# Sparse attention and two feed-forward layers on one core: later additions for pairs 12 to 15, a load on another queue, and an earlier end of odd pairs' first sums

## The chip, the cores and the metric

The program runs on one core of a Trainium2 chip. The metric is the time of one execution on the device, in microseconds (us), as the median of several runs. The trace of the kernel before is one profiled execution. Its engines are PE (TensorE; PEld is its weight load), DVE (VectorE), ACT (ScalarE), POOL (GpSimd) and SP, which computes nothing here and only issues DMAs. Every engine works through its own instructions in order, so an instruction that waits holds up all that stand behind it on that engine, the DMAs that the engine issues among them.

## The reference

Four batches of 576 tokens with 8 heads of 64 go through an attention in which only scores within `tau` of the row's maximum count. Its output is the input of a gated layer (d_ff 1536), and that one's output of a second layer (d_ff 1024) with a softmax-weighted activation and a layer norm. All of it is float32.

```python
def _attn_ref(q, k, v, tau):
    scores = (1.0 / np.sqrt(q.shape[-1])) * np.matmul(q, k.transpose(0, 1, 3, 2))
    thresh = np.max(scores, axis=-1, keepdims=True) - tau
    scores = np.where(scores >= thresh, scores, -1000000000.0)
    attn = np.exp(scores - np.max(scores, axis=-1, keepdims=True))
    attn = attn / (np.sum(attn, axis=-1, keepdims=True) + 1e-09)
    return np.matmul(attn, v)

def _moe_ref(x, w_a, w_b, w_out):          # x: attention output, 2304 x 512
    return ((x @ w_a) * (x @ w_b)) @ w_out

def _moe2_ref(x, w_in, w_out, g_ln):
    h = x @ w_in
    e = np.exp(h - np.max(h, axis=-1, keepdims=True))
    solu = h * (e / (np.sum(e, axis=-1, keepdims=True) + 1e-09))
    ln = (solu - mean(solu)) / np.sqrt(var(solu) + 1e-06) * g_ln
    return ln @ w_out
```

## The kernel before

**Attention** treats two heads at a time: 16 pairs, four of each batch, each in 9 slices of scores. The loop over `m` (78 steps) handles two slices a step, in an order written out by hand in `PROG`. In a step PE makes the scores (L684); DVE scales them and takes their maxima (`ns`, L689); ACT takes the exponential (`pe`, L701); POOL turns the maximum into a threshold (`th`, L706, 128 numbers); DVE masks by it (L715). Thresholds of the two slices stand early in a step's POOL work. PE transposes what the step before masked (L735), ACT copies it out of PSUM (`pt`, L728), and PE multiplies it with V (L787). There are no scores after step 71; steps 72 to 77 finish the last pairs.

The product with V of a pair comes in two sums, 1 and 2, which use one PSUM buffer `po` in turn. The table `PV` says in which step, counted from the pair's first, which part of which sum is multiplied: one entry for even pairs, one for odd ones. At the end of the step in which a sum is complete, ACT copies it to `xp` (L795), ahead of that step's copies `pt`. `xp` has two buffers, so pair j+2 takes the one of pair j.

**The result x** goes to DRAM (`xd`, one tensor for each batch) in two halves: SP writes the first half of a pair (L797) in the step after its second sum, and POOL later adds the second half (L798, a DMA with `accum_op=add`), behind the bulk work of its step. The addition waits until SP's write has landed. In the kernel before it is issued two steps after the pair's second sum is complete: for pairs 12, 13, 14 and 15 at the ends of steps 63, 68, 72 and 77.

**Blocks of x.** The layer after the attention takes x in three blocks of 768 columns. Block 0 (batches 0 and 1) is loaded in step 46, block 1 (batches 1 and 2) from step 65 on, both on SP: `load_z` (the reciprocal sums, L454) and `load_x` (L470, and for each new batch 512 runs of two numbers into `vs`, L473). From step 69 on, one instruction of block 1's normalization is put on DVE in each step, ahead of the step's masks; the first needs `vs`. Block 2 (the rest of batch 2 and all of batch 3, pairs 8 to 15) is loaded by SP behind the loop, with `load_x(2)`. The next instructions that SP issues then belong to the layer: stores of operands (`opd<-xt`, L554) and loads of raw weights (`wraw`, L200, two buffers). Block 2 is multiplied by its reciprocal sums much later (POOL, L492, 327.70 us).

**The gated layer** (`moe1`) runs 36 rounds of seven products each (L611) over three PSUM buffers that ACT and DVE empty. The order is planned in the program's own build by the times of a small model of the engines; `product` is called by the attention's step 72 for the first three.

Of the kernel before, what the change touches and what calls it, by code (L numbers as in the profile page):

```python
# [14 lines left out]
ALU = mybir.AluOpType  # L15
# [6 lines left out]
def kernel(  # L22
# [11 lines left out]
    nc = tc.nc  # L34
# [3 lines left out]
    S = SM + D  # L38
# [33 lines left out]
    xd = [dram.tile([P, KC, S + 2], F32, name=f"xd{b}") for b in range(B)]  # L72
# [23 lines left out]
    vs = {}  # L96
# [339 lines left out]
    def cuts(p, c0, c1):  # L436
        o, got = 0, []
        for b, s0, s1 in SEG[p]:
            a, z = max(o, c0), min(o + s1 - s0, c1)
            if a < z:  # L440
                got.append((b, s0 + a - o, a - c0, z - a))
            o += s1 - s0
        return got
# [13 lines left out]
    def alloc_x(p):  # L457
        if p == 2:
            xr = pools["w4"].tile([P, 7 * 2 * QK * P], F32, tag="w", name="x2")
            xr = xr[:, 0:KC * 2 * H].rearrange("p (k c) -> p k c", k=KC)  # L460
        else:
            xr = raw_p.tile([P, KC, 2 * H], F32, name="xr0")
        xs[p] = xr

    def load_x(p):
        if p not in xs:
            alloc_x(p)
        xr = xs[p]
        for b, s0, c, m in cuts(p, 0, 2 * H):
            nc.sync.dma_start(out=xr[:, :, c:c + m], in_=xd[b][:, :, s0:s0 + m])  # L470
            if b not in vs:
                vs[b] = const.tile([P, KC, 2], F32, name=f"vs{b}")
                nc.sync.dma_start(out=vs[b], in_=xd[b][:, :, S:S + 2])  # L473
                vnew.append(b)

    def norm_ops(p, whole=True):
# [153 lines left out]
    def attention():  # L630
        es, es_r = ExitStack(), ExitStack()
        slots, late, bulk, adds = [], [], [], []
# [21 lines left out]
        def alloc_qk(i):  # L654
            q = pq.tile([P, 2, S], F32, name="q")
            k = pq.tile([P, 2, HS + D], F32, name="k")
            ld[i] = (q, k)
# [114 lines left out]
        def pv(i, r, ka, kz):  # L772
            n = R1 if r == 1 else R2 + 2
            if ka == 0:
                st[i, "o", r] = ps_a.tile([P, 2, 512], F32, name="po", bufs=1)
            po = st[i, "o", r][:, :, 0:n]
            vr = ld[i, "v"]

            def mm(kc, h, g):
                rows = slice(g * D, (g + 1) * D)  # L780
                if kc < NQ:
                    lhsT, rhs = vr[rows, h * NQ + kc], dt[h, r][rows, kc, 0:n]
                elif g == h:
                    lhsT, rhs = vr[rows, 2 * NQ], dt["t", r][rows, 0:n]
                else:
                    return
                nc.tensor.matmul(po[h * D:(h + 1) * D, g], lhsT=lhsT, rhs=rhs, start=(kc == 0), stop=(kc == NQ - (g != h)), skip_group_check=True)  # L787

            def store():
                b, hp = divmod(i, NPAIR)  # L790
                if r == 1:
                    st[i, "x"] = px.tile([P, 2, S + 2], F32, name="xp")
                xp = st[i, "x"]
                c0 = 0 if r == 1 else R1
                nc.scalar.activation(out=xp[:, :, c0:c0 + n], in_=po, func=AF.Copy)  # L795
                if r == 2:
                    dma_q.append(lambda: nc.sync.dma_start(out=xd[b][:, hp, :], in_=xp[:, 0]))  # L797
                    adds.append((m + 2, lambda: nc.gpsimd.dma_start(out=xd[b][:, hp, :], in_=xp[:, 1], accum_op=ALU.add)))  # L798

            if kz == NQ + 1:  # L800
                pv_q.append(store)
            return [lambda kc=kc, h=h, g=g: mm(kc, h, g) for kc in range(ka, kz) for g in range(2) for h in range(2)]
# [14 lines left out]

            pv_q.append(store)

        PV = ({4: (1, 0, 3), 5: (1, 3, 5), 6: (2, 0, 2), 7: (2, 2, 5)}, {4: (1, 0, 2), 5: (1, 2, 4), 6: (1, 4, 5), 7: (2, 0, 3), 8: (2, 3, 5)})  # L820
        alloc_qk(0)
        q0, k0 = ld[0]
        def first_k(eng, h, g):
# [21 lines left out]
        tot = NP * NS  # L845
# [26 lines left out]
        for m in range(tot // 2 + 6):  # L872
            if m == 46:
                load_z(0)
                load_x(0)
                ops = {"n": [[x] for x in norm_ops(0)], "s": sum_ops(0, 0, True), "z": [[("S", 0, lambda: load_z(1))]], "x": [[("S", 0, lambda: load_x(1))]]}
                ops["h"], ops["l"] = zip(*(operand_ops(0, j, 0, True) for j in range(NX)))
                ops["o"] = [[("S", 0, lambda j=j: store_op(0, j, 0))] for j in range(NX)]
                slots = [[x for w in st.split() for x in ops[w[0]][int(w[1])]] for st in STEPS]
                late = norm_ops(1)  # L880
# [8 lines left out]
            lo_old, lo_q = lo_q, []  # L889
            pvs = [(j,) + PV[j % 2][m - j * NS // 2] for j in range(max(0, 2 * m // NS - 2), min(NP, 2 * m // NS + 1)) if m - j * NS // 2 in PV[j % 2]]  # L890
            mms = [f for p in pvs for f in pv(*p)]
# [111 lines left out]
        for fn in dma_q + [fn for _, fn in adds] + later:  # L1003
            fn()
        later.clear()
        load_x(2)
        es.close()

    yt = {}
# [456 lines left out]
    with tc.manual_schedule():  # L1466
        mhalf = const.tile([P, 1], F32, name="mhalf")
        nc.gpsimd.memset(mhalf, -0.5)
        attention()
        pools["ps"] = es_t.enter_context(tc.tile_pool(name="ps_t", bufs=4, space=PSUM))  # L1470
        pools["wo"] = ctx.enter_context(tc.tile_pool(name="wo", bufs=2 * F1))
        moe1()
        moe2()
# [56 lines left out]
```

## Time and profile before

| What | Value |
|---|---|
| Median of 3 runs | 912.55 us (912.37 to 912.76) |
| The profiled execution | 912.18 us, of which its span is 910.4 us |
| Busy in the span: PE, DVE | 880.8 us (97%), 692.0 us (76%) |
| Busy in the span: ACT, POOL | 542.4 us (60%), 175.0 us (19%) |
| Mean granted clock of TensorE | 0.994 |

The profiled execution lies 1.8 us over its span. A clock of 1.00 in a row is 2.4 GHz, 0.50 is 1.2 GHz. Attention takes the first 280 us or so of the span, the gated layer runs to about 700 us and the second layer to the end. Busy shares count an instruction from its start to its end, so PE at 97% is not PE at its peak.

### The profile page before, as it was taken

The page shows a single profiled execution, that of the slowest core. Times are in us where ns is not written, and L with a number is a line of the kernel's source. Part 1 is how long each engine was busy: PE and PEld are TensorE (multiplying, and loading weights), DVE is VectorE, ACT ScalarE, POOL GpSimd, SP SyncE. Part 2 cuts the span into 40 slices and gives each one's busy share as a digit, 9 for nine tenths or more (in the row PEclk, how much of TensorE's full clock was granted, in tenths as well). Part 3 has the DMA queues.
Part 4 walks back from the last instruction along what each step waited for, and adds up shares of the span by engine and source line. Part 5 has one row for each costly group of instructions (what it writes and reads, how often), then busy time and mean ns, then how long its engine had stood idle before and what let it go on. Part 6 is the DMA issues. An engine that isn't in the chain of part 4 may idle for free.

```text
span 910.4 us, 17279 instructions
## 1 busy us (share of the span) xinstructions
PE 880.8 (97%) x6354; PEld 742.6 (82%) x6354; DVE 692.0 (76%) x1508; ACT 542.4 (60%) x1041; POOL 175.0 (19%) x309
## 2 busy tenths in 40 slices
PE   7999999999979799999999999999999999999998
PEld 4566666656647799999999999999999778888886
DVE  6989898899966778886576755876644898888873
ACT  5899988879955464554454444544444566555543
POOL 1243542125312010001111121112114000000000
PEclk9999999999989999999999999999999999999999
DMA  6455454766754669569965998579869111110001
GB/s 176 139 150 170 109 164 130 200 184 200 220 152 142 232 211 362 168 235 367 313 159 116 251 346 274 113 176 308 250 143 197 38 35 59 47 47 24 24 23 47
DMA packets 71027, 152.50 MB, mean 168 GB/s; under 512 B 8736, under 2 KB 39072, under 8 KB 70944
## 3 DMA queue, kind: packets, MB, share of 16 engines
q1 hardware_dynamic: 57472, 131.83, 42.7%
q0 software_dynamic: 12672, 18.90, 13.8%
q8 instruction: 50, 0.82, 0.4%
q10 hardware_dynamic: 800, 0.68, 0.3%
q14 instruction: 33, 0.27, 0.1%
HBM read 98.06 MB, written 53.32 MB: 166 GB/s over the span
## 4 chain that ended last, share of the span: by engine, by line
PE 80%; DVE 7%; DMA 4%; ACT 4%; issue 2%; SPq 1%; POOL 0%; ACTq 0%; POOLq 0%; DVEq 0%
PE acc L611 26%; PE py L1130 16%; PE po L1424 10%; PE ph L1303 9%; PE po L787 6%; PE ps L684 5%; PE tp L735 5%; DVE pe L715 2%; DVE ns L689 2%; DMA xd<-xp 2%; PE pl L1401 2%; DMA xt<-opd 1%; ACT pe L701 1%; DMA wraw<-in_w_dram 1%; PE ps L769 1%
## 5 line engine op out<-in xcount | busy, mean ns | idle before, releaser
L611 PE MATMUL acc<-xt,w 128*128 128x384 f32 x1446 | 272.5, 338 | 5.6 <-ACT c L1218 2.7
L611 PEld LDWEIGHTS acc<-xt,w 128*128 128x128 f32 x1446 | 255.7, 189 | 7.2 <-DVE xt L237 3.6
L1108 POOL DMA_DIRECT2D yd<-y x68 | 58.8, 889 | 306.8 <-ACT y L1104 306.8
L701 ACT ACTIVATE pe<-ns,nm 128x576 f32<-128x576 f32 x128 | 94.3, 781 | 38.2 <-DVE ns L689 38.1
L715 DVE SCALAR_TENSOR_TENSOR pe<-ns,th,pe 128x576 f32<-128x576 f32 x128 | 100.4, 814 | 12.6 <-POOL th L706 6.4
L689 DVE TENSOR_SCALAR_CACHE_REDUCE ns<-ps 128x576 f32<-128x576 f32 x144 | 103.2, 751 | 7.4 <-PE ps L684 6.6
L1424 PE MATMUL po<-w,lt 128*128 128x512 f32 x432 | 103.5, 395 | 0.0
L684 PE MATMUL ps<-k,q 64*64 64x288 f32 x1152 | 93.6, 431 | 5.1 <-DMA k<-in_qkv_dram 3.3
L1424 PEld LDWEIGHTS po<-w,lt 128*128 128x128 f32 x432 | 79.9, 188 | 16.7
L1104 ACT ACTIVATE y<-py 128x384 f32<-128x384 f32 x92 | 45.0, 490 | 77.4 <-PE py L1130 74.4
L1130 PE MATMUL py<-ga,wo 128*128 128x384 f32 x432 | 84.0, 335 | 0.0
L1130 PE MATMUL py<-gb,wo 128*128 128x384 f32 x432 | 84.0, 335 | 0.0
L728 ACT ACTIVATE pt<-tp 128x512 f32<-128x512 f32 (+1 forms) x160 | 78.7, 556 | 2.1 <-PE tp L735 1.9
L787 PE MATMUL po<-pt,vr 64*64 64x322 f32 (+1 forms) x1024 | 77.2, 407 | 2.1 <-ACT xp L795 1.6
L1130 PEld LDWEIGHTS py<-ga,wo 128*128 128x128 f32 x432 | 75.7, 188 | 0.0
L1130 PEld LDWEIGHTS py<-gb,wo 128*128 128x128 f32 x432 | 75.7, 188 | 0.0
L1303 PE MATMUL ph<-w,ys 128*128 128x512 f32 x297 | 74.5, 394 | 0.7 <-ACT h L1307 0.7
L706 POOL TENSOR_SCALAR th<-nm,toff 128x1 f32<-128x1 f32 x144 | 49.4, 353 | 127.7 <-DVE ns L689 123.5
L735 PE MATMUL tp<-ident,pe 128*128 128x128 f32 x512 | 70.8, 280 | 0.0
L735 PEld LDWEIGHTS tp<-ident,pe 128*128 128x128 f32 x512 | 58.7, 144 | 11.0 <-issue 5.5
L684 PEld LDWEIGHTS ps<-k,q 64*64 64x64 f32 x1152 | 36.3, 136 | 37.5 <-issue 8.4
L1303 PEld LDWEIGHTS ph<-w,ys 128*128 128x128 f32 x297 | 55.7, 188 | 13.6 <-ACT h L1307 1.1
(156 smaller groups left out, 1215.4 us busy)
## 6 DMA issues: line engine op xcount, KB each, us to landing
xt<-opd SPq DMA_DIRECT2D x42, 768.0 KB
wraw<-in_w_dram SPq DMA_DIRECT2D x36, 512.0 KB
opd<-xt SPq DMA_DIRECT2D x21, 768.0 KB
yd<-y POOLq DMA_DIRECT2D x68, 192.0 KB, 5.5
q<-in_qkv_dram SPq DMA_DIRECT2D x15, 576.0 KB
k<-in_qkv_dram SPq DMA_DIRECT2D x30, 176.0 KB
xd<-xp SPq DMA_DIRECT2D x16, 289.0 KB
xd<-xp POOLq DMA_DIRECT2D x16, 289.0 KB, 5.4
```

Of the source, the lines that this page charges most:

```text
L611: nc.tensor.matmul(ps, lhsT=w[:, WOP[j], wi, c * P:(c + 1) * P], rhs=x[:, c, xi, :], start=(k == 0 and j < 3), stop=(k == 3 * QK - 1 and j ...
L684: nc.tensor.matmul(ps[t * D:(t + 1) * D, g, 0:HS], lhsT=q[r, u, c], rhs=k[r, u, o:o + HS], start=True, stop=True, skip_group_check=True)
L689: nc.vector.tensor_scalar(out=ns, in0=st[i, s][:, :, 0:HS], scalar1=-SCALE, scalar2=None, op0=ALU.mult, op1=ALU.min, accum_out=nm)
L701: nc.scalar.activation(out=pe.rearrange("p (g s) -> p g s", g=2), in_=ns, func=AF.Exp, bias=nm, scale=-1.0)
L715: last_mask[0] = nc.vector.scalar_tensor_tensor(out=pv, in0=ns, scalar=th, in1=pv, op0=ALU.is_le, op1=ALU.mult, accum_out=z[:, s:s + 1])
L728: evac_q.append(lambda: nc.scalar.activation(out=out, in_=in_, func=AF.Copy))
L735: nc.tensor.transpose(tp[:, kc, :], pe[:, o:o + P], ident)
L787: nc.tensor.matmul(po[h * D:(h + 1) * D, g], lhsT=lhsT, rhs=rhs, start=(kc == 0), stop=(kc == NQ - (g != h)), skip_group_check=True)
L1108: nc.gpsimd.dma_start(out=to[:, g["oc"], :], in_=y, accum_op=ALU.add)
L1130: nc.tensor.matmul(g["py"], lhsT=wos[g["q"] * F1 + r][:, wi, oc * P:(oc + 1) * P], rhs=g["g"][r][:, gi, :], start=(r == c == 0), stop=last ...
L1303: nc.tensor.matmul(ps, lhsT=v[:, a, c * P:(c + 1) * P], rhs=w[:, b], start=(k == 0 and j < 3), stop=(k == 3 * QK - 1 and j in (2, 4, 6)), ...
L1424: nc.tensor.matmul(po, lhsT=lt[:, a, j, :], rhs=w2(j, b), start=(k == 0), stop=(k == 3 * NJ - 1))
```

## The change

Four edits. The addition of a pair's second half of x is issued four steps after its second sum, instead of two, from step 60 on (pairs 12 and 13: ends of steps 65 and 70), and behind the loop for those complete in step 70 or later (pairs 14 and 15). `load_x(2)` is issued by GpSimd, behind these two additions. In the odd pairs the part of the first sum that was multiplied in the seventh step (the last 2 matmuls, 4 instructions) moves to the sixth, so that its copy to `xp` moves too.

```diff
-    def load_x(p):
+    def load_x(p, eng=nc.sync):
...
-            nc.sync.dma_start(out=xr[:, :, c:c + m], in_=xd[b][:, :, s0:s0 + m])
+            eng.dma_start(out=xr[:, :, c:c + m], in_=xd[b][:, :, s0:s0 + m])
...
-                nc.sync.dma_start(out=vs[b], in_=xd[b][:, :, S:S + 2])
+                eng.dma_start(out=vs[b], in_=xd[b][:, :, S:S + 2])
...
-                    adds.append((m + 2, lambda: nc.gpsimd.dma_start(out=xd[b][:, hp, :], in_=xp[:, 1], accum_op=ALU.add)))
+                    adds.append((m + (2 if m < 60 else 4) if m < 70 else tot, lambda: nc.gpsimd.dma_start(out=xd[b][:, hp, :], in_=xp[:, 1], accum_op=ALU.add)))
...
-        PV = (..., {4: (1, 0, 2), 5: (1, 2, 4), 6: (1, 4, 5), 7: (2, 0, 3), 8: (2, 3, 5)})
+        PV = (..., {4: (1, 0, 2), 5: (1, 2, 5), 7: (2, 0, 3), 8: (2, 3, 5)})
...
-        load_x(2)
+        load_x(2, nc.gpsimd)
```

## Rows read from the trace of the kernel before

**Rows 1.** Page, part 4: shares of the chain that ended last, by engine.

```profile
PE 80%; DVE 7%; DMA 4%; ACT 4%; issue 2%; SPq 1%; POOL 0%; ACTq 0%; POOLq 0%; DVEq 0%
```

**Rows 2.** Chain of waits, 170 to 345 us: start, us, what.

```profile
249.90 8.16 DMA xd<-xp
...
290.36 7.92 DMA wraw<-in_w_dram
...
300.59 5.98 PE acc L611 x24
...
317.34 4.16 PE acc L611 x24
```

**Rows 3.** Timeline, POOL: start, us, instruction, [idle before <- what ended it].

```profile
234.37 0.89 POOL L798 DMA_DIRECT2D xd<-xp  x1
...
240.58 1.00 POOL L237 TENSOR_TENSOR xt<-xr,xt 128x384 fp32r<-128x384 f32 x1 [1.44 <-DVE pe L715]
...
258.60 0.89 POOL L798 DMA_DIRECT2D xd<-xp  x1 [9.87 <-DMA xd<-xp]
```

**Rows 4.** Timeline, DVE, 225 to 310 us, the same columns.

```profile
235.61 0.82 DVE L715 SCALAR_TENSOR_TENSOR pe<-ns,th,pe 128x576 f32<-128x576 f32 x1 [0.44 <-POOL th L706]
...
255.57 0.23 DVE L480 TENSOR_SCALAR vs<-vs,neg 128x8 f32<-128x8 f32 x1 [3.92 <-DMA vs<-xd]
...
259.85 0.82 DVE L715 SCALAR_TENSOR_TENSOR pe<-ns,th,pe 128x576 f32<-128x576 f32 x1 [3.00 <-POOL th L706]
...
283.52 0.69 DVE L223 SCALAR_TENSOR_TENSOR st_a<-wraw,st_a 128x512 uint32<-128x512 uint32 x1
```

**Rows 5.** Timeline, SP's DMA queue: start, us spent issuing, what is issued.

```profile
243.00 2.77 SPq L473 DMA_DIRECT2D vs<-xd  x1
...
249.90 0.39 SPq L797 DMA_DIRECT2D xd<-xp  x1
...
281.95 6.41 SPq L470 DMA_DIRECT2D x<-xd  x2
...
290.36 0.83 SPq L200 DMA_DIRECT2D wraw<-in_w_dram  x2
```

**Rows 6.** Windows: length, busy us (count) PE PEld DVE ACT POOL, clock, DMA share, GB/s.

```profile
254.00:256.00 2.00, 2.00 (x28) 0.90 (x20) 0.43 (x2) 0.02 (x1) 0.00 (x0) 1.00 0.99 388
...
260.00:262.00 2.00, 0.00 (x0) 0.00 (x0) 2.00 (x5) 0.00 (x0) 0.04 (x1) 0.50 1.03 145
...
300.00:304.00 4.00, 3.41 (x11) 3.41 (x12) 2.55 (x7) 2.42 (x5) 0.00 (x0) 0.57 0.02 8
```

**Rows 7.** Tile xd: time from issue to landing of the DMAs on POOL's queue.

```profile
DMA to landing us min/median/max: 4.1/5.4/8.1
```

**Rows 8.** Timeline, ACT, 225 to 310 us.

```profile
249.74 0.59 ACT L795 ACTIVATE xp<-po 128x512 f32<-128x512 f32 x1
...
298.36 0.66 ACT L216 ACTIVATE st_a<-wraw 128x512 f32<-128x512 f32 x1 [3.44 <-DMA wraw<-in_w_dram]
```

**Rows 9.** Timeline, PE, 225 to 310 us.

```profile
274.76 0.65 PE L787 MATMUL po<-ptt,vr 64*64 64x256 f32 x4
...
276.11 2.40 PE L787 MATMUL po<-pt,vr 64*64 64x322 f32 x32 [0.70 <-ACT xp L795]
...
300.59 6.14 PE L611 MATMUL acc<-xt,w 128*128 128x384 f32 x25 [2.71 <-ACT c L1218]
```

**Rows 10.** Waits of PE's weight loads, 20 to 250 us: us, times, longest.

```profile
PEld po L787 <- ACT xp L795: 4.8, 9, 1.1
```

**Rows 11.** Timelines, PEld and ACT, in step 37, where pair 7 ends its first sum.

```profile
136.85 0.86 PEld L735 LDWEIGHTS tp<-ident,pe 128*128 128x128 f32 x8 [0.38 <-ACT pt L728]
...
138.97 1.29 PEld L787 LDWEIGHTS po<-pt,vr 64*64 64x64 f32 x24 [0.40 <-ACT xp L795]
...
136.98 1.46 ACT L701 ACTIVATE pe<-ns,nm 128x576 f32<-128x576 f32 x2 [0.21 <-DVE ns L689]
```

**Rows 12.** Timeline, DVE, in step 28, where pair 5 ends its first sum.

```profile
106.54 0.82 DVE L715 SCALAR_TENSOR_TENSOR pe<-ns,th,pe 128x576 f32<-128x576 f32 x1 [0.98 <-ACT pe L701]
```

More of the change, by code (lines that the diff above doesn't have):

```diff
@@ L818, in finish @@
             pv_q.append(store)
-        PV = ({4: (1, 0, 3), 5: (1, 3, 5), 6: (2, 0, 2), 7: (2, 2, 5)}, {4: (1, 0, 2), 5: (1, 2, 4), 6: (1, 4, 5), 7: (2, 0, 3), 8: (2, 3, 5)})
+        PV = ({4: (1, 0, 3), 5: (1, 3, 5), 6: (2, 0, 2), 7: (2, 2, 5)}, {4: (1, 0, 2), 5: (1, 2, 5), 7: (2, 0, 3), 8: (2, 3, 5)})
         alloc_qk(0)
```

## The prediction, made before the changed kernel was run

> **What bounds the kernel now.** First the page's chain: by engine, 80% of it is PE, and only DVE, DMA and ACT have a few per cent each [rows 1]. So time can come only from places where PE stops. The chain in order of time says where: around the end of the attention it runs through a write of x, 8.16 us, and a load of raw weights, 7.92 us [rows 2]. Then the waits there, engine by engine.
>
> First stop, step 68 to 69: POOL stood 9.87 us in front of pair 13's addition, until SP's write of that pair had landed [rows 3]. That write was issued at 249.90, because SP had been held in its queue by block 1's loads (the issue of `vs` alone took 2.77 us), and landed 8.16 us later [rows 2, 5]. Behind the addition stood step 69's thresholds, and DVE waited 3.00 us for them. But this is the second wait of that step: just before, DVE had waited 3.92 us for `vs`, until 255.57 [rows 4]. Taking the addition away gives back 3.00 us, not 9.87.
>
> Second stop, 298 to 300 us: SP's `load_x(2)` took from 281.95 to 288.36, since its second part waits for pair 15's addition, and the weights behind it were issued at 290.36 only [rows 5]. ACT waited 3.44 us for them, and PE, for a copy behind that on ACT, 2.71 us [rows 8, 9]. The clock then fell to a mean of 0.57 over the next 4 us [rows 6]: 24 products took 5.98 us there and 4.16 us later [rows 2].
>
> Third, short stops on `xp`, between a pair's two sums: 9 of them, 4.8 us in all, on PE's weight loads up to 250 us [rows 10], and 0.70 us at 276.11 [rows 9].
>
> **The change part by part**, against the 912.18 us of the profiled execution.
>
> *Pair 13's addition, to step 70.* DVE's 3.00 us go, if `vs` lands as before. The write lands at 249.90 + 8.16 = 258.06 [rows 2], before even step 70's own thresholds, so POOL does not stop at the end of step 70, and step 71's thresholds wait for their own maxima anyway. *Pair 12's addition, from step 63 to 65*, though, is moved into the stretch in which block 1 is loaded and the DMA engines are full (share 0.99 still at 254 to 256); alone, an addition takes a share of 1.03 of 2.00 us, so 2.06 us of all engines [rows 6]. The transfers of block 1 have a backlog until `vs` lands, so the `vs` wait can grow by 0 to 2.06 us, and the gain is 3.00 to 0.94. I take 2.0 of delay, near the full price, since the addition is issued behind step 65's bulk work (240.58 + 1.00 = 241.6 [rows 3]), before the issue of `vs` ends (245.77 [rows 5]), and the engines stay full until it lands: **-1.0**. PE stands still behind this (nothing from 260 to 262, clock 0.50 [rows 6]); of that pause most is left, so I count nothing for the clock.
>
> The Trainium skill ("DMA: Bandwidth & Descriptors", section on queues, rings and completion order) says that each DMA engine takes turns between the queues that have work, packet by packet. By that, an addition on GpSimd's queue does not line up behind SP's backlog, and SP pays the whole price, which speaks against this edit; were it served last, `vs` would be as before and the gain 3.0. No row decides between the two.
>
> In the step behind an addition, DVE's mask waits 0.44 us for its threshold (step 64) [rows 4]. That price moves from step 64 to 66. In step 64 the copy `xp`, now earlier on ACT, holds the mask up about as long (next part), so I count the move as **+0.4**; the bounds are 0 and 0.44. Pair 14's copy at 249.74 [rows 8] takes the `xp` buffer of pair 12. Even at the longest landing, 8.1 us [rows 7], 241.6 + 8.1 is 249.7, and a stop of ACT of up to some 3 us is covered by DVE's wait for `vs`: nothing.
>
> *Pairs 14 and 15's additions behind the loop.* Pair 14's had no threshold behind it (the last are those of step 71): nothing. Pair 15's stands behind it, at its old place in POOL's order otherwise: less than 1 us later, with nothing but the load behind it.
>
> *`load_x(2)` on POOL.* What is now queued behind it on POOL is block 2's multiplication (L492), tens of us later; nobody waits for that block sooner: nothing. SP goes on from 281.95 at once: the store of an operand, then the first weights, whose buffer is read until 283.52 + 0.69 = 284.21 [rows 4]. In the changed kernel that is 282.9 (1.3 us sooner by the next part). With the old 7.92 us they land at 290.8. Beside them now run two additions (4.1 us of all engines) and the first part of x (128 x 4 x 192 numbers, 0.4 MB) instead of the second (128 x 4 x 576, 1.2 MB), behind which they lay; at the 388 GB/s of [rows 6] that is 4.1 + 1.0 - 3.1 = 2.0 us more: 292.8. ACT wants them at 298.36 - 3.44 = 294.92 [rows 8], less 1.3: 293.6. They come in time, with under a microsecond to spare by this harsh count. PE gets 2.71 back, and without the pause the clock's 5.98 - 4.16 = 1.82: **-4.5**. Bounds: 0 and -4.5; if a remnant of the pause still lowers the clock, -2.7. What is late next is DVE's share of operand splits, which moves along.
>
> *First sums of odd pairs, the last one.* For pair 15 the 4 instructions at 274.76 (0.65 us, behind the first products) go into step 72, where PE waits for DVE's mask anyway, and the wait of 0.70 us for their copy goes [rows 9]: **-1.3**. ACT's copy and SP's write move up with it.
>
> *The seven others.* At best PE's waits for `xp` go: 4.8 us over 9 [rows 10], so 0.53 each, -3.7. But ACT's copy, 0.59 us [rows 8], now stands at the end of the step before, ahead of `pt`. In pair 7, PE's transposes already wait 0.38 us for that `pt`, and ACT has 0.21 us to spare before the next exponential [rows 11]: PE's 0.40 us wait for `xp` becomes a longer wait for `pt`, about level, with 0.59 - 0.21 = 0.38 more for DVE's mask, of which PE's later slack takes most. In pair 5 ACT has nothing to spare, and DVE's mask waits 0.98 us for the exponential [rows 12]: the whole copy adds. Pairs 1 and 5 +0.5 each, 7 and 9 +0.1 each, 3, 11 and 13 nothing (3 has DVE work in front of the mask, 11 ACT idle; 13 is counted above): **+1.2**. Bounds: -3.7 and 7 x 0.59 = +4.1.
>
> Sum: -1.0 + 0.4 - 4.5 - 1.3 + 1.2 = -5.2. 912.18 - 5.2 = **907.0 us**. The profiled execution is 0.4 us under the median, which I leave inside the range.
>
> **Rivals.** (1) *The short prices are not paid*: `vs` lands as before (-3.0), and ACT's early copies are hidden (0 for 0.4 + 1.2). 912.18 - 3.0 - 4.5 - 1.3 = 903.4. For it: an addition could be served last. Against: the engines are full until `vs` lands. (2) *The weights are late again*: the additions and x share the engines with the first weights, and a wait of ACT takes the place of the old one. 907.0 + 4.5 = 911.5; half late, about 909.5. For it: under a microsecond to spare. (3) *Slower*: pair 12's addition holds back block 1's loads by much more than its own work. From a delay of `vs` of 3.0 us step 69 gains nothing; each further us costs one, so against the 2.0 of the forecast the whole is slower than 912.18 from 7.2 us on, and by over 0.2% from 9.4. If the 12.6 us from the issue of `vs` at 243.00 to 255.57 were doubled by turns, the delay is 12.6 and the time 907.0 + 10.6 = 917.6. For it: an addition has landed after as much as 8.1 us [rows 7]. Against: its work is 2.06 us. (4) *The wait only moves* to step 71 with pair 13's addition, because the write lands later still: then the gain of 1.0 there is lost: 908.0.
>
> **How the numbers follow.** The forecast with (4), which is near it: 0.60. Rival 1: 0.16. Rival 2: 0.19, a third of it faster by over 0.2%. Rival 3: 0.05. Range: from 902.5, under rival 1, to 911.5, rival 2; the best bound of the odd pairs and rival 3 are left out, with the worst of rival 2, together 2 in 10. 0.2% is 1.8 us, about what a measurement of this kernel can tell from no change: faster is under 910.7, slower over 914.4. Faster 0.60 + 0.16 + 0.06 = 0.82, same 0.13, slower 0.05.
>
> **What would show it.** Right: no idle time on POOL ahead of pair 13's addition; DVE's wait for `vs` some 2 us longer, and its wait for the threshold in step 69 gone; weights issued within 2 us of SP's last write of x; no wait of PE near 297 us, and the clock at 1.00 in the 4 us behind it; PE's 36 products of pair 15's second sum straight behind the first products. Wrong: a wait of ACT for `wraw`, or a wait of DVE for the threshold of steps 69 to 71; odd pairs' steps before 235 us shorter or longer by more than 0.5 us a pair. With 36 rounds behind all this in which PE hardly stops, what is gained or lost by 310 us should stand at the end.

## The result, and the profile after

| What | Before | After |
|---|---|---|
| Median of 5 runs | 912.55 us (911.39 to 914.56) | 905.06 us (903.84 to 905.83) |
| Ratio, 95% interval | | 0.9915 (0.990 to 0.9931) |
| Span of the profiled execution | 910.4 us | 902.9 us |
| Mean granted clock | 0.994 | 0.998 |

The change makes the kernel 7.5 us faster, by the medians and by the spans (the two profiled executions, 912.18 and 905.06, are 7.1 apart); 907.0 us was forecast, with a range of 902.5 to 911.5. The sign, the main cause and the range held, but 1.9 us were missed, and several of the terms behind the number were off. The views of the kernel after show most of it.

The chain of waits, 240 to 290 us (start, us, what). Before, it ran through a write of x, 8.16 us, and the raw weights, 7.92 us [rows 2].

```profile
242.09 11.20 DMA xd<-xp
...
279.52 4.83 DMA xd<-xp
284.35 2.07 issue
286.50 0.63 ACT wo L243
```

The raw weights are gone from it. In their place stand two additions: that of pair 12, issued at 242.09, which took 11.20 us to land, and that of pair 15, behind which ACT wrote the tile `wo`. The prediction counted what waits behind either at nothing. (The 2.07 us of "issue" are time to which this view gives no cause; the addition itself landed later than the chain puts it, as the runs below show.) The landing times of `xd` on POOL's queue (before: 4.1, 5.4 and 8.1 [rows 7]):

```profile
DMA to landing us min/median/max: 4.1/6.3/11.2
```

What each engine waited for. The timelines of DVE, ACT and PE (start, us, instruction, [idle before <- what ended it]):

```profile
243.34 0.82 DVE L715 SCALAR_TENSOR_TENSOR pe<-ns,th,pe 128x576 f32<-128x576 f32 x1 [0.91 <-POOL th L706]
...
257.45 0.23 DVE L480 TENSOR_SCALAR vs<-vs,neg 128x8 f32<-128x8 f32 x1 [4.86 <-DMA vs<-xd]
```

```profile
253.32 0.60 ACT L795 ACTIVATE xp<-po 128x512 f32<-128x512 f32 x1 [2.35 <-DMA xd<-xp]
...
286.50 0.63 ACT L243 ACTIVATE wo<-st_a 128x512 fp32r<-128x512 f32 x1 [2.15 <-DVE c L1211]
```

```profile
254.24 1.59 PE L787 MATMUL po<-pt,vr 64*64 64x322 f32 x16 [2.51 <-ACT pt L728]
...
272.82 2.40 PE L787 MATMUL po<-pt,vr 64*64 64x322 f32 x32
...
287.97 1.32 PE L611 MATMUL py<-xt,w 128*128 128x384 f32 x6 [0.70 <-ACT c L1218]
...
301.34 1.14 PE L611 MATMUL acc<-xt,w 128*128 128x384 f32 x5 [1.34 <-DVE xt L237]
```

Against [rows 4], [rows 8] and [rows 9]: DVE's mask of step 69 no longer waits 3.00 us for a threshold, its wait for `vs` grew from 3.92 to 4.86, and step 66's mask has a wait of 0.91. ACT's wait of 3.44 us for `wraw` and PE's of 2.71 behind it are gone. New is ACT's wait of 2.35 us for pair 14's `xp` buffer, and the one before `wo` is 2.15 us, of which 0.70 reaches PE. The row names DVE as what ended the 2.15 us; the runs below show that it was an addition. In the kernel before, the same instruction waited 0.23 us; that row of ACT, and PE's first products behind the late weights there, are:

```profile
287.80 0.63 ACT L243 ACTIVATE wo<-st_a 128x512 fp32r<-128x512 f32 x1 [0.23 <-issue]
```

```profile
308.07 1.14 PE L611 MATMUL acc<-xt,w 128*128 128x384 f32 x5 [1.34 <-DVE xt L237]
```

POOL and SP's queue:

```profile
242.09 0.89 POOL L798 DMA_DIRECT2D xd<-xp  x1
...
262.22 0.89 POOL L798 DMA_DIRECT2D xd<-xp  x1
...
278.71 1.78 POOL L798 DMA_DIRECT2D xd<-xp  x2
...
286.93 0.79 POOL L470 DMA_DIRECT2D x<-xd  x1 [5.75 <-DMA xd<-xp]
```

```profile
238.87 2.61 SPq L454 DMA_DIRECT2D sc<-rzd  x4
...
281.10 4.98 SPq L200 DMA_DIRECT2D wraw<-in_w_dram  x2
```

Pair 13's addition (262.22) has no wait in front of it, against 9.87 us [rows 3]. The weights are issued at 281.10, not 290.36 [rows 5]. The wait for pair 15's addition is still there, 5.75 us, but it now stands on POOL, in front of the second part of x, with nothing behind it that anyone needs soon.

Windows (columns as in [rows 6]):

```profile
256.00:258.00 2.00, 2.00 (x12) 1.63 (x15) 0.55 (x2) 1.05 (x3) 0.00 (x0) 0.50 0.99 396
...
260.00:262.00 2.00, 2.00 (x24) 1.25 (x17) 2.00 (x7) 1.08 (x2) 0.53 (x2) 1.00 0.01 2
...
296.00:304.00 8.00, 6.66 (x38) 6.33 (x38) 7.31 (x14) 5.15 (x9) 0.00 (x0) 1.00 0.53 195
```

The clock of 0.57 behind 300 us [rows 6] is 1.00. The half clock near the end of the attention is still there, but sooner: 0.50 at 256 to 258, where DVE waits for `vs` until 257.45 in any case, and 1.00 at 260 to 262, where it was 0.50.

An account by the starts of the same instructions in both traces, as the after minus before in us: +0.94 at step 69, -1.21 at step 70, -1.95 at the first products, -3.29 at pair 15's second sum, -2.36 at the products behind `wo` (287.97), -6.73 at the products behind the new weights (301.34), -7.5 at the end. The two executions differ by 0.39 already in steps 6 to 9, before any edit acts. Over the traces of all the runs below, the first maxima of step 9 stand from 0.80 us ahead of the kernel before to 0.40 behind it, so differences of up to a microsecond between starts in two traces can be the executions' own; where it matters, a start is read against an earlier one of the same trace. These are the first maxima of steps 9 and 50 before:

```profile
38.20 0.75 DVE L689 TENSOR_SCALAR_CACHE_REDUCE ns<-ps 128x576 f32<-128x576 f32 x1
...
180.53 0.76 DVE L689 TENSOR_SCALAR_CACHE_REDUCE ns<-ps 128x576 f32<-128x576 f32 x1 [0.20 <-PE ps L684]
```

And after, where the stretch between them is 1.28 us longer:

```profile
37.81 0.74 DVE L689 TENSOR_SCALAR_CACHE_REDUCE ns<-ps 128x576 f32<-128x576 f32 x1
...
181.42 0.76 DVE L689 TENSOR_SCALAR_CACHE_REDUCE ns<-ps 128x576 f32<-128x576 f32 x1 [0.20 <-PE ps L684]
```

### The profile page after: what moved, and what is told of

Same layout as the page of the kernel before. It is cut to its first block, busy times and chain, and to the rows that moved or that the text cites. A ratio compares the mean times of both kernels' runs of the same rounds, so it can differ in the third digit from the quotient of the medians.

```text
span 902.9 us, 17281 instructions
## 1 busy us (share of the span) xinstructions
PE 879.7 (97%) x6354; PEld 740.6 (82%) x6354; DVE 691.6 (77%) x1508; ACT 542.3 (60%) x1041; POOL 178.9 (20%) x312
## 4 chain that ended last, share of the span: by engine, by line
PE 82%; DVE 7%; ACT 4%; issue 3%; DMA 2%; POOL 1%; ACTq 0%; DVEq 0%; POOLq 0%
PE acc L611 27%; PE py L1130 16%; PE po L1424 10%; PE ph L1303 9%; PE po L787 6%; PE ps L684 5%; PE tp L735 5%; DVE ns L689 2%; DVE pe L715 2%; DMA xd<-xp 2%; PE pl L1401 2%; ACT pe L701 1%; PE ps L769 1%; POOL w L237 1%; ACT pt L728 1%
```

## The experiments

Medians of different jobs are compared by their ratio to the kernel before, which ran beside each.

### The three edits, one at a time

**The earlier end of the odd pairs' first sums alone.**

```diff
-        PV = (..., {4: (1, 0, 2), 5: (1, 2, 4), 6: (1, 4, 5), 7: (2, 0, 3), 8: (2, 3, 5)})
+        PV = (..., {4: (1, 0, 2), 5: (1, 2, 5), 7: (2, 0, 3), 8: (2, 3, 5)})
```

> The kernel before with the odd pairs' first sums ended a step sooner, nothing else. Theory (the account from the two traces): ACT's earlier copy adds about 0.5 us in pairs 1 and 5 and 0.1 in two others, so step 66's first maximum comes 0.6 to 1.0 us later than before; pair 15's second sum then starts 1.3 us sooner behind the first products; together 911.9 to 912.4 us. Rival (the early copies are hidden, only PE's waits on xp go): steps up to 66 level or up to 3 us sooner, 908 to 911.2 us.

Measured: 912.22 us, ratio 0.9993 (0.9984 to 1.0003). By step 66 the kernel is 1.0 us later than before (1.4 counted from step 9). Pair 15's second sum has no wait left and stands 3.31 us behind the first products, where it stood 4.67 behind them, so 1.36 comes back. Then the stop for the weights follows as before, but not the clock. Timeline of PE and a window of this run:

```profile
301.36 4.63 PE L611 MATMUL acc<-xt,w 128*128 128x384 f32 x25 [3.21 <-ACT c L1218]
```

```profile
300.00:304.00 4.00, 2.64 (x15) 2.64 (x16) 3.30 (x7) 3.32 (x7) 0.00 (x0) 1.00 0.08 34
```

What follows: the seven other odd pairs cost, pair 15 gains, and the two cancel, as the terms +1.2 and -1.3 said. The stop of PE before 301.36 is longer than the 2.71 us of the kernel before [rows 9], yet the clock stayed at 1.00. So the 1.82 us that the prediction took for the clock are a price that such a stop can have, not one that it must have.

**The four later additions alone.**

```diff
-                    adds.append((m + 2, ...))
+                    adds.append((m + (2 if m < 60 else 4) if m < 70 else tot, ...))
```

> The kernel before with the four later additions, nothing else. Theory: step 67 about 0.7 us later (threshold behind pair 12's addition), step 70 about 2.1 us sooner against step 69, ACT waiting 2 to 3 us for the xp buffer without cost; then SP's load of block 2 waits for two additions instead of one, and PE's stop near 298 us grows from 2.7 to about 3.7 us: 911 to 912 us. Rival (the additions behind the loop cost nothing): the 2.0 us gained at 268 us stand at the end, 910.5 us.

Measured: 911.26 us, ratio 0.9981 (0.9971 to 0.9992). Step 70 starts 2.84 us sooner than before and the first products 3.6 us sooner (0.65 of it was there in step 9, before any edit acts); 1.6 us are left at the end of the trace. Timelines of ACT, PE and SP's queue:

```profile
251.72 0.60 ACT L795 ACTIVATE xp<-po 128x512 f32<-128x512 f32 x1 [1.94 <-DMA xd<-xp]
...
297.18 0.66 ACT L216 ACTIVATE st_a<-wraw 128x512 f32<-128x512 f32 x1 [5.31 <-DMA wraw<-in_w_dram]
```

```profile
299.41 6.21 PE L611 MATMUL acc<-xt,w 128*128 128x384 f32 x25 [4.58 <-ACT c L1218]
```

```profile
278.37 7.88 SPq L470 DMA_DIRECT2D x<-xd  x2
...
288.08 0.92 SPq L200 DMA_DIRECT2D wraw<-in_w_dram  x2
```

What follows: DVE's wait for the threshold in step 69 goes, as forecast, and ACT's wait for the `xp` buffer comes with the later additions alone, behind pair 12's (240.91 to 251.72, 10.8 us). But two microseconds are given back at the second stop: with both additions behind the loop, SP's load of x takes 7.88 us, held by them, the weights are issued 2.3 us sooner only, and PE, which is 3.6 us ahead, waits 4.58 us for them, where about 3.7 were expected. This edit needs the other queue for the load.

**The load of block 2 on GpSimd alone.**

```diff
-        load_x(2)
+        load_x(2, nc.gpsimd)
```

> The kernel before with block 2 loaded by GpSimd, nothing else. Theory: everything up to 282 us as before; weights issued near 284 us, ACT does not wait for them, PE's stop of 2.71 us near 298 and the half clock behind it are gone: 4.5 us, and up to 0.5 us near 420: 907.5 to 908 us. Rival (the load and the addition share the engines with the weights, which land as late as before): 911 to 912.5 us.

Measured: 907.75 us, ratio 0.9939 (0.9924 to 0.9954). SP's queue and PE:

```profile
283.70 5.04 SPq L200 DMA_DIRECT2D wraw<-in_w_dram  x2
```

```profile
303.13 1.15 PE L611 MATMUL acc<-xt,w 128*128 128x384 f32 x5 [1.33 <-DVE xt L237]
```

What follows: up to 282 us this is the kernel before, within 0.8. The weights are issued at 283.70, ACT doesn't wait for them, and the products that started at 308.07 start at 303.13: -4.94, of which 0.6 were there at the first products (270.84 against 271.44). That leaves -4.3, so the term of -4.5 is shown, and by the ratios (0.6, 1.7 and 5.6 us of 912.55 for the three edits, 7.8 for all) it is most of the gain. The three parts add up to the whole within their intervals. One price shows here already: ACT's `wo` waits 1.25 us (288.26), where it waited 0.23 before, though no addition was moved; none of it reaches PE in this run.

### What the change left on the table

**The earlier end for pair 15 alone**, the other odd pairs as before, all else as after.

```diff
-        PV = (even, odd)
+        PV = tuple((even, odd_before)[j % 2] for j in range(NP - 1)) + (odd,)
```

> The changed kernel, with the earlier end of the first sum for pair 15 alone; the other odd pairs as before. Theory: the seven early copies cost about 1.0 us up to step 66, so 904.0 us, step 66 level with the kernel before. Rival (they cost nothing that lasts, since a later wait takes it up): 905.1 us.

Measured: 904.85 us, ratio 0.991 (0.9895 to 0.9926), beside 0.9915 for the kernel after; its span is 1.3 us shorter (901.6).

What follows: the time does not decide between 904.0 and 905.1 us, since the two intervals overlap. The traces do. From the first maxima of step 9 to those of step 50, where five of the seven pairs are through, each of the five traces so far and below in which all odd pairs end early is 1.27 to 1.45 us longer than the kernel before, and the six others are between 0.05 shorter and 0.21 longer. So the early copies cost what the term said (+1.2). Step 66 does not show it as well: this run stands 0.94 us ahead of the kernel before there, where after is 0.58 behind, but 0.78 of the 0.94 was there in step 9, and between steps 50 and 55 the traces drift apart by about a microsecond, whichever table they run.

**Pair 12's addition at step 63 again**, all else as after.

```diff
-                    adds.append((m + (2 if m < 60 else 4) if m < 70 else tot, ...))
+                    adds.append((m + (2 if m < 65 else 4) if m < 70 else tot, ...))
```

> The changed kernel with pair 12's addition back at step 63. Theory (the moved addition costs a threshold wait of 0.9 us in step 66 and 0.5 to 0.9 us of the wait for vs; ACT's wait of 2.35 us for the xp buffer that it holds costs nothing, since DVE waits for vs): no wait of ACT for xp, the wait for vs 3.8 to 4.0 us instead of 4.9, first products about 1 us sooner than 269.5; 903.5 to 904.5 us. Rival (the wait for the xp buffer costs its 2.35 us too): first products 3 us sooner, 902 us.

Measured: 905.48 us in one run, above the 903.5 to 904.5 that were expected. Timelines of DVE, POOL and ACT:

```profile
256.33 0.23 DVE L480 TENSOR_SCALAR vs<-vs,neg 128x8 f32<-128x8 f32 x1 [3.30 <-DMA vs<-xd]
```

```profile
277.75 1.79 POOL L798 DMA_DIRECT2D xd<-xp  x2
...
286.89 0.79 POOL L470 DMA_DIRECT2D x<-xd  x1 [6.67 <-DMA xd<-xp]
```

```profile
286.47 0.63 ACT L243 ACTIVATE wo<-st_a 128x512 fp32r<-128x512 f32 x1 [3.08 <-issue]
```

What follows: ACT's wait for the `xp` buffer and the wait of step 66 are gone, and `vs` lands sooner: this run was 0.94 us behind the kernel after at step 66 (0.79 of it since step 9) and is 0.94 ahead of it at the first products (268.55 to 269.49), so the early addition gives 1.9 us there. None of it reaches the end of this run. ACT's `wo` starts where it did (286.47; 286.50 after), idle 3.08 us instead of 2.15, and PE's products behind the weights at 301.31 (301.34 after).

**Pair 14's addition at step 72**, all else as after.

```diff
-                    adds.append((... if m < 70 else tot, ...))
+                    adds.append((... if m < 70 else m + 2 if m < 75 else tot, ...))
```

> The changed kernel with pair 14's addition back at step 72. Theory (the first write into wo, behind the attention, waits for both additions, and PE behind it 0.70 us): ACT's wait there falls from 2.15 to 1.3 us or less, PE's 0.70 us goes, 904.2 us. Rival (it waits for pair 15's addition alone, which lands no sooner): both waits as in the changed kernel, 905 us.

Measured: 904.65 us in one run, which cannot tell 904.2 from 905. Pair 14's addition is issued at 268.61. POOL and ACT:

```profile
280.25 0.88 POOL L798 DMA_DIRECT2D xd<-xp  x1 [0.74 <-DMA xd<-xp]
...
286.79 0.78 POOL L470 DMA_DIRECT2D x<-xd  x1 [4.91 <-DMA xd<-xp]
```

```profile
286.36 0.63 ACT L243 ACTIVATE wo<-st_a 128x512 fp32r<-128x512 f32 x1 [1.33 <-DVE st_t L223]
```

What follows: what `wo` waits for is pair 15's addition. ACT's start there and POOL's start of the second part of x, which waits for that addition, are 0.42 or 0.43 us apart in all nine traces in which POOL issues that load (286.50 and 286.93 after; 286.47 and 286.89 above; 286.36 and 286.79 here). In all twelve traces, the kernel before among them, ACT starts `wo` 0.15 us after that addition has landed (after: issued at 279.52, landed at 286.35; before: 282.82 and 287.65). By the program, `wo` lies in memory that held the attention's `xp`, and this instruction waits for the additions that read it. From its own issue the addition takes 4.8 us to land before, 5.9 with the load of x on GpSimd as the only edit, 6.0 here, and behind pair 14's, as one group, 6.8 after and 7.8 above. So both edits made it later: the load and the weights, which now run beside it, and the group. From the start of the group to `wo` it is 7.8 us after (278.71 to 286.50), and 8.7 above; from pair 15's issue alone it is 6.1 here. Why the group took longer above than after is open. PE's wait of 0.70 us at 288 is gone, and the run, 0.75 us behind the kernel after at the first products, is level with it at 301.22.

**Block 1's normalization from step 70**, all else as after, so that DVE's wait for `vs` moves a step later.

```diff
-                    elif m >= 69 or m >= tot // 2:
+                    elif m >= 70:
```

> The changed kernel with the normalization of block 1 begun in step 70 instead of 69 (its fourth instruction stays in step 72). Theory (DVE's wait for vs in step 69 is now the largest stop): it moves behind step 69's masks, and shrinks by what DVE does in between; the xp wait of ACT, till now covered, decides step 69 then, its masks come near 256 instead of 258.65 us; 902 to 903 us. Rival (the wait only moves into step 70 and holds up step 71 as long): 905 us.

Measured: 905.37 us, ratio 0.9916 (0.990 to 0.9932): no change against after, and the 905 of the rival, not the 902 to 903 of the theory. DVE, PE and two windows:

```profile
255.28 0.82 DVE L715 SCALAR_TENSOR_TENSOR pe<-ns,th,pe 128x576 f32<-128x576 f32 x1 [2.88 <-ACT pe L701]
```

```profile
253.81 1.92 PE L787 MATMUL po<-pt,vr 64*64 64x322 f32 x16 [2.25 <-ACT pt L728]
...
287.66 1.32 PE L611 MATMUL py<-xt,w 128*128 128x384 f32 x6 [1.74 <-ACT c L1218]
```

```profile
256.00:258.00 2.00, 2.00 (x12) 1.54 (x14) 0.84 (x4) 0.87 (x2) 0.00 (x0) 0.50 0.99 392
...
290.00:291.00 1.00, 1.00 (x5) 1.00 (x4) 0.72 (x2) 0.26 (x2) 0.00 (x0) 0.50 0.94 373
```

What follows: with `vs` out of the way, the wait of ACT for the `xp` buffer (2.10 us here) is late next, and DVE waits 2.88 us for the exponential behind it. So in the kernel after that wait was covered by the one for `vs`, as the prediction said of such a stop, and is worth its own time once the cover is gone. What is gained against after by the first products, 1.3 us (268.21), is more than lost at `wo`: PE stops 1.74 us there, the clock falls behind it (0.50), and the products behind the weights start at 302.60, against 301.34.

### The four together, and two of them taken out again

Pair 15 alone with the early first sum, pair 12's addition at step 63, pair 14's at step 72, the normalization from step 70.

> The changed kernel with what the theory says is better: pair 12's addition in step 63, pair 14's in step 72, the early end of the first sum for pair 15 alone, the normalization of block 1 from step 70. Theory: the sum of the parts, against 905: 1.0 (early copies), 1.3 (pair 12), 0.7 (pair 14) and 2 to 4 (the wait for vs, which no wait for xp replaces): 898 to 900 us. Rival (the wait for vs only moves a step): 902 us.

Measured: **898.65 us** (897.91 to 898.94), ratio **0.984** (0.9824 to 0.9857): 14.6 us under the kernel before by the ratio, and 6.8 under the kernel after. DVE, POOL, ACT and one window over the whole stretch:

```profile
252.48 0.82 DVE L715 SCALAR_TENSOR_TENSOR pe<-ns,th,pe 128x576 f32<-128x576 f32 x1 [0.49 <-POOL th L706]
...
255.91 0.23 DVE L480 TENSOR_SCALAR vs<-vs,neg 128x8 f32<-128x8 f32 x1
```

```profile
274.39 0.88 POOL L798 DMA_DIRECT2D xd<-xp  x1 [0.74 <-DMA xd<-xp]
...
280.98 0.78 POOL L470 DMA_DIRECT2D x<-xd  x1 [4.96 <-DMA xd<-xp]
```

```profile
280.55 0.63 ACT L243 ACTIVATE wo<-st_a 128x512 fp32r<-128x512 f32 x1 [1.35 <-DVE st_t L223]
```

```profile
244.00:300.00 56.00, 52.04 (x437) 42.05 (x430) 49.41 (x99) 37.75 (x74) 14.52 (x20) 1.00 0.71 221
```

What follows: the edits that did next to nothing alone do much together. The reading is that each took away one of two or three waits that ended at nearly the same time; the next two runs test it for two of the four, and what pair 14's addition and the early end for pair 15 alone are worth in the combination was not tried. `vs` is there when DVE comes to it (no idle time at 255.91), `wo` starts 6.2 us after the issue of pair 15's addition (274.39 to 280.55) and PE doesn't wait for it, and the clock is 1.00 from 244 to 300. The first products start at 264.39, where the kernel after has 269.49.

**Without the later normalization** (from step 69 again, the other three kept).

```diff
-                    elif m >= 70:
+                    elif m >= 69 or m >= tot // 2:
```

> The combination without one of its edits: block 1's normalization starts in step 69 again (pair 12's addition at step 63, pair 14's at step 72, early first-sum end for pair 15 alone). Theory: the steps up to 69 run ahead, and the landing of vs does not, since it is set by block 1's transfers; so DVE waits some 3 us for vs in step 69 (3.30 in the run with pair 12's addition early, plus what the steps run ahead), PE stops over 2 us near 253 us, and the time is 2.5 to 4.5 us above the combination's 898.65: 901 to 903. Rival: the later normalization is worth little and the combination's gain comes from the other edits: below 900.

Measured: 902.48 us, ratio 0.9882 (0.9858 to 0.9906). DVE and PE:

```profile
256.68 0.23 DVE L480 TENSOR_SCALAR vs<-vs,neg 128x8 f32<-128x8 f32 x1 [3.96 <-DMA vs<-xd]
```

```profile
260.17 0.54 PE L769 MATMUL ps<-ident,pe 128*128 128x128 f32 x2 [3.07 <-DVE ns L689]
```

What follows: as expected, the landing of `vs` is what DVE meets in step 69, and a step more on DVE covers it. PE's stop is at 260.17, though, not near 253 us, where it was expected. The edit that was worth nothing on the kernel after is worth 3.8 us here, by the ratios.

**Without the early addition of pair 12** (step 65 again, the other three kept).

```diff
-                    adds.append((m + (2 if m < 65 else 4) if m < 70 else ...))
+                    adds.append((m + (2 if m < 60 else 4) if m < 70 else ...))
```

> The combination without another of its edits: pair 12's addition is issued at step 65 again (normalization from step 70, pair 14's addition at step 72, early first-sum end for pair 15 alone). Theory: ACT waits about 2 us for pair 12's xp buffer at 251 to 253 us, as in the run with the normalization moved alone, and since DVE's wait for vs no longer covers it, DVE's mask in step 68 waits 2 to 3 us for the exponential behind it; so 901 to 902.5. Rival: some other part of the combination hides the wait of ACT, or the addition lands in time with the odd pairs' copies as before: below 900.

Measured: 900.72 us, ratio 0.987 (0.9848 to 0.9892). ACT and DVE:

```profile
252.29 0.60 ACT L795 ACTIVATE xp<-po 128x512 f32<-128x512 f32 x1 [2.07 <-DMA xd<-xp]
```

```profile
254.69 0.82 DVE L715 SCALAR_TENSOR_TENSOR pe<-ns,th,pe 128x576 f32<-128x576 f32 x1 [2.86 <-ACT pe L701]
```

What follows: both waits came as expected, 2.07 and 2.86 us. The time is 0.3 us under the range that was expected; by the ratios pair 12's early addition is worth 2.7 us, with intervals that overlap slightly, and by the spans (898.6 and 897.1) 1.5. So its sign rests on the waits in the traces, its size is open between these.

## Why the prediction was right, point by point

| Term | Forecast, us | By the two traces, us |
|---|---|---|
| Seven odd pairs, and the threshold wait of step 66 | +1.6 | +0.94 (+1.33 from step 6 on) |
| Step 69 | -1.0 | -2.15 |
| Step 70 to the first products | 0 | -0.74 |
| Pair 15's second sum | -1.3 | -1.34 |
| The write of `wo` | 0 | +0.87 |
| The weights' stop | -4.5 | -4.37 |
| All behind 302 us | 0 | -0.77 |
| Sum | -5.2 | -7.5 |

The remaining movement, 0.06 us between pair 15's second sum and `wo`, makes up the difference of the column. The total lies about as near to rival 1 (903.4) as to the forecast (907.0), but not by that rival's mechanism: `vs` did land later, and the early copies did cost. What was missed in both directions cancelled in part, and that the total stayed in the range owes something to luck.

*The seven odd pairs, and step 66*: +1.2 came out, 1.27 to 1.45 us by step 50 in five traces. The +0.4 for step 66 was too low, and its upper bound of 0.44 too: in each of the six traces with pair 12's addition at step 65 the first maxima of step 67 lose 0.66 to 0.69 us against those of step 66, and in the five others nothing. What the move saves in step 64, 0.41 us by step 65, shows only in the three of the six without the early copies, as forecast.

*The weights*: right in cause and size. The weights were issued at 281.10, within 2 us of the forecast 282.9, but not within 2 us of SP's last write of x (276.89, so 4.2), the sign that the prediction named: its own times, 282.9 and 280.2 less 1.3, did not fit that sign either. The additions and x beside them did not make them late, so rival 2 fell. The share of 1.82 us for the clock was right for this pair of kernels, but the first experiment shows a stop of 3.21 us without it: the forecast had luck there.

*Step 69*: the mechanism was right (the 3.00 us go, `vs` comes later), the size of the delay was mis-sized. I took 2.0 us. From the first load of block 1 (`sc`) to DVE's first use of `vs` it is 17.27 us before (238.30 to 255.57) and 18.58 after (238.87 to 257.45), so 1.31. In the other traces in which DVE waits for `vs` it is 17.12, 17.15, 17.33 and, once, 16.52 us with pair 12's addition at step 63 (the first, third, ninth and fifth experiment), and 18.33, 18.38 and 18.56 with it at step 65 (the second, fourth and sixth). So this step failed in a size, 1.31 for 2.0. A second, smaller fault was to add the price of step 66 on top. Block 1's loads were issued 0.57 later than before and DVE came to the wait 0.94 later; the 0.37 between the two stand inside the wait for `vs`, so that wait grew by 1.31 - 0.37 = 0.94 only (4.86 against 3.92). Delays that run side by side to the same wait were added up there. The Trainium skill's rule that queues take turns ("DMA: Bandwidth & Descriptors", section on queues, rings and completion order), from which the whole 2.06 us came out as SP's price, is not borne out in full by the 1.31; nor is the other end, at which SP would pay nothing.

*The `xp` buffer*: "nothing" was right for the time and wrong in its ground. I allowed up to 8.1 us of landing, the longest row of before [rows 7]; it was 11.2, and ACT stopped for 2.35 us. The cover that I named, DVE's wait for `vs`, held: from DVE's first use of `vs` to the first products it is 12.04 us in the four traces with both waits, and 12.22 and 12.44 in the fifth and ninth experiment, which have no stop of ACT. The run with the normalization a step later and the last run show what it costs without it.

*Step 70 to the first products*: counted as nothing, since I left most of PE's pause and the clock behind it in place. The pause came sooner instead (2.51 us up to 254.24; before, PE still stood at 260 to 262 [rows 6]), so the stretch at half clock fell beneath the wait for `vs`, and the clock was 1.00 at 260 to 262. That the 0.74 us are this was not tried apart, but other traces agree: the 12.04 us from `vs` to the first products are the same after and in the second and fourth experiment, where the clock stayed at 1.00 from 248 to 270, and the 12.22 and 12.44 belong to traces in which the half clock came at 260 to 264, behind that wait.

*`wo`*: missed. I asked who waits behind the moved additions on POOL's queue, and found the load of x. I did not ask who writes to the memory that they read. ACT's first write to `wo` already waited 0.23 us for pair 15's addition in the kernel before, and that addition then took 2 us longer to land (4.8 before, 6.8 after): 1.1 with the load of x on GpSimd as the only edit, the rest behind pair 14's addition.

*Pair 13's addition, pair 15's second sum, rival 3 and rival 4*: the first two came out as forecast, the rivals did not come. No idle time stands ahead of the addition at 262.22, pair 15's second sum follows the first products without a wait, the delay of `vs` is far from the 7.2 us from which rival 3 decides, and DVE has no wait for a threshold in steps 69 to 71. What held pair 13's write on SP in the kernel before was not only the issue of `vs`, as the prediction has it: the issue of an operand's store behind it took longer still, and why is open.

```profile
245.81 3.99 SPq L554 DMA_DIRECT2D opd<-xt  x1
```

*Behind 302 us*: 0.77 us more came by the end, against a forecast of none. 0.48 of it stands near 420 us, where a wait of PE for a stored operand (0.22 us in its row) is gone; the rest was not followed up and stays open.

## What to carry to other kernels

When a wait is taken away, look for the waits that ended just before it on the same path: each of the last four edits alone moved the kernel after by half a microsecond at most, and together they took 6.8 off, since a wait taken away alone mostly showed the next. When a DMA is moved, ask not only what is queued behind it, but also which later instruction writes to the memory that it reads, or that was put where it lay. And two delays that end in the same wait are not added: what arrives late at a wait has paid part of it.

## What the runs showed of the hardware

An accumulating DMA of 289 KB that was issued while the DMA engines were full (0.99 still at 256 to 258 in the kernel after) took 10.8 to 11.3 us to land in the six traces that have it, against a median of 5.4 in the kernel before, and the loads beside it took 1.31 us longer (after against before): it paid more for the crowd than the crowd paid for it.

Around the end of the attention the granted clock fell from 2.4 to 1.2 GHz behind stops of PE of 1.74 and 2.25 us (normalization later), 2.41 (pair 12's addition at step 63), 2.51 (after), 2.60 (pair 14's at step 72), 2.71 (before), 3.07 (normalization from step 69 again) and 4.58 (the additions alone), and behind those of 6.00 to 6.23 near 262 us in the kernel before and two other runs. It stayed up behind 1.63 (pair 12's addition at step 63), 2.09 (the additions alone), 2.16 (pair 15 alone), 2.23 (the last run) and 3.21 us (the first). So the length of the stop alone doesn't decide it in these runs; what does was not tried.
